# Transposing x of the last four half batches by DMA, in an attention and token-mixing kernel

## The chip, the core and the metric

The kernel runs on one core of a Trainium2 chip. The metric is the device time of one launch in microseconds. The kernel before was run three times: 123.89, 124.62 and 125.48 us, a median of 124.62.

## The reference

Linear attention with a cosine weighting of positions, and then a mixing of tokens whose weights are computed from the attention's output. B = 8 batches, H = 8 heads, S = 576 positions, D = 64, all inputs and the output in fp32.

```python
theta = np.pi / 2.0 * np.arange(S) / S
phi(x) = concat(relu(x) * cos(theta), relu(x) * sin(theta))        # per head, 128 features
kv  = einsum('bhsf,bhsd->bhfd', phi(k), v)
z   = sum(phi(k), axis=2)
num = einsum('bhsf,bhfd->bhsd', phi(q), kv)
den = einsum('bhsf,bhf->bhs', phi(q), z)[..., None] + 1e-06
x   = (num / den), heads side by side                              # B, S, 512
wq, wk = x @ w_q, x @ w_k                                          # B, S, 64
W_tok  = einsum('bsd,btd->bst', wq, wk) / sqrt(64)
out    = relu(einsum('bst,btd->bsd', W_tok, x)) @ w_out            # B, S, 512
```

The kernel never forms `W_tok`: since `W_tok @ x = wq @ (wk^T @ x)`, it computes `wk^T @ x` (64 x 512) for each batch.

## The kernel before, in words

The work of attention is cut into 16 half batches H = 0 to 15. Half batch H is batch H // 2 and four of its heads, as two pairs of heads. Each pair gives one group g = 2H or 2H + 1, so that there are 32 groups. The mixing runs once for each of the 8 batches, and the last product, by `w_out`, in 36 row tiles of 128 rows.

The order of all work is written out by hand in the string `ORDER` (line 24). Each word is a step and its index, then `:` and the place in PSUM, then `@` and the engine that copies (A for ScalarE, V for VectorE, G for GpSimd). Each engine, and each queue of transfers, does its part of the words in the order in which they stand. All transfers are issued from SyncE's queue (SP). An SP instruction that must wait holds back all that stand behind it there.

The steps that matter here, with their lines:

- `LK`, `LQ`, `LV` (`load`, line 129) bring in k, q and v, two transfers of 288 KB for each half batch. The last loads in the order are those of `LK15`.
- `N` (line 261) computes numerators and denominators of one group into PSUM, `EP` (274) adds 1e-06 to the denominators, and `X` (281) on VectorE takes the reciprocal (L286) and multiplies (L287) into the bf16 buffer `x`. `x` has two buffers, one for a batch and one for the next. Its layout is partition, `u` (5 blocks of two 64-row pieces), head, d.
- `XT` (292) and `XR` (303) transpose `x` on TensorE into PSUM. `XT` moves whole 128 x 128 blocks, 10 for a half batch (L300). `XR` moves halves of 64 partitions, 20 for a half batch (L313). Both are followed by `XE` (316), which copies the result from PSUM into the bf16 buffer `xT`, on ScalarE (L193) or VectorE (L197).
- `WK` (328) takes `xT` of both half batches of one batch, 20 matmuls (L333), and `KW` copies the result to `wk`. `KX` (355) computes `wk^T @ x` with 10 matmuls, whose moving operand is 256 columns of `x` (L360). `WQ` (341) takes `xT` as moving operand (L346). `MX` (378) and `ME` mix and apply the relu.
- `WO` (398) computes one row tile with 4 matmuls of 512 columns (L403), `OE` (406) copies it to one of 12 output buffers `o`, and `ST` (412) stores it, 256 KB each (L413).

The half batches 12 to 15 are the last four. They form the batches 6 and 7. In the order, `XR12` stands behind `N27`, and `XR13` behind `QT14`. `XE12` and `XE13` are on ScalarE, and `WK6` follows `WO19`. `XR14` and `XR15` stand together behind `X31`, the last `X`. `MX27`, `WO25` and `WK7` follow.

Of the kernel before, what the change touches and what calls it, by code (L numbers as in the profile page):

```python
# [13 lines left out]
BF16 = mybir.dt.bfloat16  # L14
# [7 lines left out]


ORDER = """
LV1 LQ0b LQ1 TK CV1@G TQ LK1 TV LV0a TI TZ LV0b T2 RK1@G RQ1@A TW VS1 LK0a CV0b@A QT1:0 RQ0b@A
LQ0a CV0a@G KV1:2 LK0b RK0a@G RQ0a@A QM1 KE1@V RK0b@A VS0a VS0b N2:4 LV3 LQ3 RQ3@A LK3 CV3@G EP2@V
N3:6 LV2 LK2 QT0:0 KV0:2 X2 EP3@A LQ2 RK3@G QM0 KE0@A VS3 N0:4 LV5 X3 QT3:0 EP0@A KV3:2 QM3 LW0
LW1 X0 CV2@G KE3@A RK2@A VS2 XT1:6 N1:0 EP1@A LK5 LQ4 X1 N6:4 CV5@G LQ5 XE1@A RQ2@A EP6@A LV7 N7:2
LV4 KV2:0 QT2:6 EP7@A LQ7 KE2@V XT0:0 X6 CW1 QM2 CW0 N5:4 XE0@A WK0:6 N4:0 RK5@A X7 RQ5@G WQ0:7
VS5 EP4@V X4 EP5@V KW0@A RQ4@A KX0:6 XR3:2 XK0@A QW0@V X5 XB0@A XE3@A XA0@A KV5:0 LK4 LQ6 KE5@A  # L30
QT5:6 LW2 XT2:4 CV7@G MX1:2 QM5 LV6 XE2@A MX3:0 QT4:6 CV4@G ME1@A ME3@A RK4@G MX2:4 VS4 LK7 QM4
WK1:2 WQ1:3 KW1@A N11:0 RQ7@G KX1:2 CW3@G N10:6 QW1@V ME2@A MX0:4 XK1@A EP11@A ME0@A VS7 X11 KV4:2
EP10@A KE4@A N9:4 X10 N8:0 RQ6@A CW4@G XT5:2 EP8@A X8 LV8 LK6 CV6@G RK7@G QT7:6 LV10 CW2@A EP9@A
X9 XA1@A CW5@A WO1:0 XE5@A LQ8 LV9 XR4:4 QT6:2 WO2:1 QM7 OE1:0@A KV7:6 XB1@G QM6 RK6@G VS6 XE4@A
MX7:2 WQ2:0 KE7@A MX4:4 ME7@A OE2:1@A N15:6 MX5:2 QW2@A ME4@V EP15@A WK2:1 N14:4 LK10 ME5@A KW2@A
KV6:2 EP14@A X15 CV8@G KE6@A MX6:0 ME6@A KX2:6 LQ9 X14 N12:2 VS8 LK8 XK2@A EP12@A N13:0 EP13@A X13
CV9@G WO7:7 RQ8@A XR7:4 QT8:0 OE7:2@A WO0:6 XE7@A XA2@G X12 RQ9@G LK9 WO5:7 OE0:3@A WO4:6 VS9
XB2@A MX9:4 QM8 XR6:2 OE5:4@A LQ11 RK8@A QT9:0 CV10@G WO6:7 RK9@G RQ11@G OE4:5@A LV11 CV11@G ME9@V
MX11:4 XE6@V KV8:2 LQ10 WK3:6 ME11@A MX10:4 OE6:6@A QM9 KV9:0 VS10 KW3@A RK10@G ME10@A KE9@A KE8@V
KX3:7 XK3@A ST6 MX8:4 XB3@V N19:0 LK11 EP19@V N18:2 ME8@A N16:6 WO11:4 LV12 RQ10@G WO3:5 X19  # L40
QT11:0 EP18@A EP16@A X18 N17:2 OE11:7@A WQ3:4 X16 XA3@A OE3:8@A EP17@A QW3@A KV10:6 X17 RK11@G
KE10@A QM11 XR9:4 CV12@G LK14 QT10:2 QM10 WO9:6 XE9@A LK13 XT8:0 WO12:7 WO8:2 OE9:9@A XE8@A WK4:3
LV13 VS11 MX12:4 OE12:10@A MX13:0 VS12 OE8:11@A N20:6 KW4@A LQ12 KV11:2 ME12@A ME13@A CV13@G
EP20@V LK12 KE11@A WO10:4 N22:0 MX15:2 X20 VS13 OE10:6@A EP22@A ME15@A MX14:6 KX4:5 WQ4:4 N23:2
RQ12@G ME14@A LQ13 XK4@A RK12@A RK13@G N21:6 EP21@A X22 XA4@G QW4@A ST10 XB4@G WO13:5 LV14 LV15
EP23@V X23 OE13:6@A KV12:0 ST13 ST4 X21 KE12@A KV13:2 LQ14 KE13@A MX17:4 ME17@A QT12:6 QM12 XR11:0
XR10:2 XE11@A RQ13@G WO17:4 QT13:6 ST3 MX16:0 LQ15 WO15:5 CV15@G ME16@A CV14@G N25:0 XE10@V ST11
OE15:6@A N24:2 QM13 ST15 EP25@V OE17:5@A MX19:6 X25 EP24@A WQ5:5 ST17 LK15 QW5@A WO14:4 RQ14@G
WK5:5 ME19@A X24 MX18:0 N27:6 XR12:2 OE14:8@A KW5@A ST5 ME18@A VS15 RQ15@G EP27@A RK15@G N26:4
KX5:0 XK5@A EP26@V WO18:1 WO16:0 X27 X26 QT15:6 QT14:4 XE12@A OE16:7@A XR13:2 WO20:0 OE18:6@A ST8  # L50
RK14@G VS14 XE13@A QM14 WO19:1 QM15 ST7 WK6:2 OE20:5@A XB5@A KV15:4 XA5@G KW6@A KV14:6 ST20 MX23:2
OE19:4@V KE15@A MX21:0 ST0 WQ6:4 ME21@A KE14@V KX6:5 ME23@V MX20:0 N30:6 MX22:2 QW6@V WO21:4
ME20@A N29:0 EP30@V ST2 ME22@A XK6@A N28:2 X30 N31:6 EP29@A EP28@A X29 X28 OE21:11@A ST12 XB6@A
WO24:5 XA6@G WO22:4 OE24:2@A WO23:5 EP31@A X31 OE22:5@A XR14:0 XR15:2 XE14@A MX27:6 OE23:3@V
WO25:4 ST18 XE15@V ST16 WK7:5 ME27@V OE25:1@A MX26:0 KW7@A ME26@A MX25:2 ST14 MX24:6 WQ7:4 KX7:5
ME24@V ME25@A WO26:0 XK7@A QW7@V XB7@A WO29:1 MX31:6 XA7@G ST22 MX28:2 ME31@A ST9 MX30:4 OE26:10@V
WO28:0 ST21 MX29:6 ST23 ST1 ME30@A OE29:6@V WO30:1 ST25 ME29@A ST19 ME28@V ST29 OE28:7@V WO32:0
ST24 WO31:4 ST26 ST28 WO33:5 OE32:8@V OE30:5@A ST32 ST30 OE31:9@A ST31 OE33:11@A WO27:6 OE27:3@A
ST33 WO35:7 ST27 OE35:0@A ST35 WO34:2 OE34:1@A ST34
"""  # L60


# [1 line left out]
def kernel(  # L64
# [10 lines left out]
    nc = tc.nc  # L75

    B, NH, S, D = q.shape
    DM = NH * D
    DH = moe_w_q.shape[1]
    P = 128  # L80
# [4 lines left out]
    SC = CP // 2  # L85
    HS = S // 2
    NDM = DM // P
# [6 lines left out]
    NRAW, NPREP, NV2, NQM, NX, NXT, NOUT = (4, 2, 2, 2, 2, 2, 12)  # L94
    XC = DM // 2
# [5 lines left out]
    def bufs(n, shape, dtype, name):  # L101
        return [pool.tile(shape, dtype, name=f"{name}{i}") for i in range(n)]
# [6 lines left out]
    qm_b = bufs(NQM, [P, 2, 2, CP, D], BF16, "qm")  # L109
    kv_b = bufs(2, [P, 2, 2, DV], BF16, "kvs")  # L110
    rec_b = bufs(8, [P, 2, SC, 1], FP32, "rec")
    x_b = bufs(NX, [P, SC, NH, D], BF16, "x")
    xT_b = bufs(NXT, [P, NDM, CP, D], BF16, "xT")
    wk_b = bufs(2, [P, SC, DH], BF16, "wk")
    wq_b = bufs(2, [P, HS], BF16, "wq")
# [23 lines left out]
    ident = pool.tile([P, P], BF16, name="ident")  # L139
# [42 lines left out]
    A, V, G = nc.scalar, nc.vector, nc.gpsimd  # L182
# [35 lines left out]
    def pair(i):  # L218
        return PS[:, i:i + 2, :]
# [38 lines left out]
    def num(t):  # L258
        return pair(t).bitcast(FP32)[:, :, 0:SC * (D + 1)].rearrange("p w (u e) -> p w u e", u=SC)
# [21 lines left out]
    def X(g, ps, eng):  # L281
        H, r = divmod(g, 2)
        b, h = divmod(H, 2)
        rec = rec_b[g % 8]
        nv = num(place["N", g])
        V.reciprocal(rec, rec)  # L286
        V.tensor_tensor(  # L287
            x_b[b % NX][:, :, 4 * h:4 * h + 4, :].rearrange(
                "p u (w r) d -> p r w u d", r=2)[:, r],
            nv[:, :, :, 0:D], rec.to_broadcast([P, 2, SC, D]), op=ALU.mult)  # L290

    def XT(H, ps, eng):
        b, h = divmod(H, 2)
        o = pair(ps).rearrange("p t e -> p (t e)").bitcast(BF16)[:, 0:2 * SC * P].rearrange(
            "p (w n) -> p w n", w=2)
        place["XT", H] = o[:, :, 0:S]
        for w in range(2):
            for u in range(SC):
                hd = 4 * h + 2 * w
                nc.tensor.transpose(o[:, w, u * P:(u + 1) * P],  # L300
                                    x_b[b % NX][:, u, hd:hd + 2, :], ident)

    def XR(H, ps, eng):
        b, h = divmod(H, 2)
        o = pair(ps).bitcast(BF16)[:, :, 0:2 * SC * D].rearrange(
            "p t (w u d) -> p w t u d", w=2, d=D)
        place["XT", H] = o
        for w in range(2):
            for u in range(SC):
                for t in range(2):  # L310
                    a = slice(H2 * t, H2 * t + H2)
                    hd = 4 * h + 2 * w
                    nc.tensor.transpose(o[:, w, t, u, :], x_b[b % NX][a, u, hd:hd + 2, :],  # L313
                                        ident[a, a])

    def XE(H, ps, eng):
        b, h = divmod(H, 2)
        dst = xT_b[b % NXT][:, 2 * h:2 * h + 2]
        o = place["XT", H]
        if len(o.shape) == 5:  # L320
            cast(eng, dst.rearrange("p w (u t) d -> p w t u d", t=2), o)
        else:
            cast(eng, dst[:, :, 0:C, :].rearrange("p w c d -> p w (c d)"), o)

    def bank(i):
        return PS[:, i, :].bitcast(FP32)
# [28 lines left out]
    def KX(b, ps, eng):  # L355
        place["KX", b] = ps
        o = bank(ps)
        for u in range(SC):
            for t in range(2):
                nc.tensor.matmul(  # L360
                    o[H2 * t:H2 * t + H2, 0:XC], wk_b[b % 2][:, u, :],
                    x_b[b % NX][:, u].rearrange("p h d -> p (h d)")[:, t * XC:(t + 1) * XC],
                    start=(u == 0), stop=(u == SC - 1))

    def XK(b, ps, eng):
# [57 lines left out]
    def CW(i, ps, eng):  # L423
        if i < 2:
            cast(eng, (wqw, wkw)[i], (wq_f, wk_f)[i])
        else:
            m = i - 2
            cast(eng, wow[:, m, :], wo_f[:, m, :])

    steps = {f.__name__: f for f in (KV, QT, KE, QM, N, EP, X, XT, XR, XE, WK, KW, WQ, QW, KX, XK, XA, XB,  # L430
                                     MX, ME, WO, OE, ST, LW, CW, TK, TV, TI, TQ, TW, T2, TZ)}
    halves = {f.__name__: f for f in (RK, RQ, CV, VS)}

    for word in ORDER.split():
        word, _, eng = word.partition("@")
        word, _, ps = word.partition(":")
# [3 lines left out]
        i, ps = int(word[len(kind):] or 0), int(ps or 0)  # L440
# [37 lines left out]
```

## Time and profile before

| | |
|---|---|
| median of three runs | 124.62 us |
| profiled execution, its own time | 122.49 us |
| span of that execution, first to last instruction | 120.7 us |
| granted TensorE clock, mean of the core | 0.991 |
| TensorE matmuls busy | 94.8 us (79%) |
| VectorE busy | 88.2 us (73%) |
| ScalarE busy | 84.2 us (70%) |
| GpSimd busy | 52.2 us (43%) |
| moved by DMA | 39.40 MB, mean 326 GB/s |
| XR's matmuls (L313) | 220, of 191 ns |
| copies into `xT` from XR | 8 on ScalarE of 1229 ns, 3 on VectorE of 817 ns |
| median from issue to landing of a store | 3.1 us |

Busy times are those of one profiled execution. Matmuls overlap each other, so that a group's busy time is less than its count times the mean of one. The lines `SPq` of a timeline are the issuing of transfers by SyncE, not the transfers themselves. The DMA share is the mean busy share of the core's 16 DMA engines, and it can lie a little above 1.

### The profile page before, as it was taken

The numbers are of one execution on the slowest core, as the hardware profiler recorded it, in microseconds if no ns is written. First come the engines' busy times: TensorE is split into PE (matmuls) and PEld (weight loads), VectorE is DVE, ScalarE is ACT, GpSimd is POOL, SyncE is SP. The second block draws the span as 40 slices with busy tenths as digits, with TensorE's granted clock in tenths as the row PEclk, the third lists the DMA queues.
The fourth block names the chain that finished last, engine by engine and source line by source line (L and its number), as shares of the span: only waits on it lengthen the run. The fifth ranks groups of instructions, "written<-read, shape, count | busy, mean of one in ns | idle before, by whom it ended". The sixth has DMA issues, their size and how long they took to land.

```text
span 120.7 us, 5301 instructions
## 1 busy us (share of the span) xinstructions
PE 94.8 (79%) x2286; PEld 63.1 (52%) x2286; DVE 88.2 (73%) x132; ACT 84.2 (70%) x155; POOL 52.2 (43%) x63
## 2 busy tenths in 40 slices
PE   0005919758778899969999999798999999999950
PEld 0004818637656656635667576454755864653410
DVE  0136998889989998997979987759969868766200
ACT  7246452967887989777967897586678668757450
POOL 2577136032739758146799304937365310010000
PEclk9999999999999999999999999999999999999996
DMA  3999999999999999999989999999997681875685
GB/s 111 318 384 405 395 391 391 361 405 396 392 390 408 398 337 344 355 360 379 383 282 326 364 285 391 343 331 283 391 299 263 238 329 55 320 288 198 237 331 196
DMA packets 20615, 39.40 MB, mean 326 GB/s; under 512 B 3184, under 2 KB 3184, under 8 KB 20592
## 3 DMA queue, kind: packets, MB, share of 16 engines
q1 hardware_dynamic: 20592, 39.07, 89.8%
q8 instruction: 18, 0.29, 1.0%
q14 instruction: 5, 0.04, 0.1%
HBM read 29.62 MB, written 9.44 MB: 324 GB/s over the span
## 4 chain that ended last, share of the span: by engine, by line
DMA 39%; PE 39%; DVE 6%; issue 4%; SPq 3%; ACT 3%; POOL 2%; DVEq 0%; ACTq 0%; POOLq 0%
DMA kraw<-in_k_dram 24%; PE ps L403 20%; DMA vraw<-in_v_dram 11%; DMA out_dram<-o 5%; PE ps L234 3%; PE ps L383 3%; PE ps L269 3%; SPq L132 3%; PE ps L360 3%; DVE v L213 2%; PE ps L313 2%; DVE x L287 2%; PE ps L245 2%; PE ps L333 2%; PE ps L346 2%
## 5 line engine op out<-in xcount | busy, mean ns | idle before, releaser
L403 PE MATMUL ps<-wow,mix 128*128 128x512 bf16 x144 | 34.7, 380 | 0.0
L287 DVE TENSOR_TENSOR x<-ps,rec 128x640 bf16<-128x640 f32 x32 | 26.4, 824 | 2.2
L195 POOL TENSOR_SCALAR vb<-vraw 128x1152 bf16<-128x1152 f32 (+1 forms) x16 | 17.9, 1122 | 20.9 <-DMA vraw<-in_v_dram 18.6
L213 DVE TENSOR_TENSOR v<-vb,vtab 128x2304 bf16<-128x2304 bf16 (+1 forms) x17 | 21.7, 1289 | 6.6 <-POOL vb L195 6.6
L253 DVE TENSOR_TENSOR qm<-ps,qtab 128x2304 bf16<-128x2304 bf16 x16 | 21.4, 1350 | 4.6 <-ACT qtab L166 2.9
L193 ACT COPY o<-ps 128x512 f32<-128x512 f32 x30 | 17.5, 587 | 6.6 <-PE ps L403 4.5
L269 PE MATMUL ps<-kvs,qm 64*128 64x65 bf16 x640 | 15.3, 199 | 6.0 <-ACT kvs L193 3.3
L403 PEld LDWEIGHTS <-mix 128*128 128x128 bf16 x144 | 12.4, 98 | 14.2 <-issue 0.9
L394 ACT ACTIVATE mix<-ps 128x576 bf16<-128x576 f32 x26 | 16.4, 657 | 3.2 <-PE ps L383 3.2
L189 POOL TENSOR_SCALAR rq<-qraw 128x1152 bf16<-128x1152 f32 x9 | 13.4, 1487 | 11.4 <-DMA qraw<-in_q_dram 10.8
L269 PEld LDWEIGHTS <-qm 64*128 64x128 bf16 x640 | 13.3, 100 | 9.4 <-issue 5.7
L189 POOL TENSOR_SCALAR rk<-kraw 128x1152 bf16<-128x1152 f32 (+1 forms) x12 | 13.8, 1150 | 9.4 <-DMA kraw<-in_k_dram 7.0
L193 ACT COPY xT<-ps 128x1280 bf16<-128x1280 bf16 (+1 forms) x13 | 15.4, 1186 | 3.3 <-PE ps L313 1.7
L234 PE MATMUL ps<-v,rk 64*64 64x130 bf16 x576 | 12.5, 236 | 3.0 <-DVE x L287 1.3
L245 PE MATMUL ps<-ident,rq 64*128 64x64 bf16 x288 | 7.6, 199 | 9.3 <-ACT rq L187 8.8
L187 ACT ACTIVATE rq<-qraw 128x1152 bf16<-128x1152 f32 (+1 forms) x8 | 8.4, 1046 | 6.6 <-DMA qraw<-in_q_dram 6.6
L234 PEld LDWEIGHTS <-rk 64*64 64x64 bf16 x576 | 10.1, 117 | 5.2 <-ACT rk L187 1.4
L245 PEld LDWEIGHTS <-rq 64*128 64x128 bf16 x288 | 6.1, 101 | 11.7 <-ACT rq L187 9.0
L383 PE MATMUL ps<-wq,kx 64*128 64x288 bf16 x64 | 8.3, 287 | 0.3 <-ACT xT L193 0.2
L195 POOL TENSOR_SCALAR kx<-kx 64x256 bf16<-64x256 bf16 x7 | 2.8, 399 | 12.6 <-ACT kx L193 12.2
L286 DVE RECIPROCAL rec<-rec 128x10 f32<-128x10 f32 x32 | 6.8, 211 | 1.8 <-ACT rec L277 1.4
L277 ACT ACTIVATE rec<-ps,eps 128x10 f32<-128x10 f32 x23 | 6.2, 273 | 1.7 <-PE ps L269 1.6
(46 smaller groups left out, 99.3 us busy)
## 6 DMA issues: line engine op xcount, KB each, us to landing
vraw<-in_v_dram SPq DMA_DIRECT2D x32, 288.0 KB, 6.0
qraw<-in_q_dram SPq DMA_DIRECT2D x32, 288.0 KB, 5.9
kraw<-in_k_dram SPq DMA_DIRECT2D x32, 288.0 KB, 5.9
out_dram<-o SPq DMA_DIRECT2D x36, 256.0 KB, 3.1
wof<-in_moe_w_out_dram SPq DMA_DIRECT2D x1, 1024.0 KB, 7.6
wqf<-in_moe_w_q_dram SPq DMA_DIRECT2D x1, 128.0 KB, 5.5
wkf<-in_moe_w_k_dram SPq DMA_DIRECT2D x1, 128.0 KB, 5.2
```

Source lines behind the costliest of these rows:

```text
L189: eng.tensor_scalar(dst, s, FMAX, 0.0, op0=ALU.min, op1=ALU.max)
L193: A.copy(dst, s)
L195: G.tensor_scalar(dst, s, 1.0, 1.0, op0=ALU.mult, op1=ALU.mult)
L213: V.tensor_mul(v2_b[H % NV2][:, part, :, :, 0:D], vb_b[H % NPREP][:, part].unsqueeze(3).to_broadcast([P, n, C, 2, D]), vtab.unsqueeze(1).t ...
L234: nc.tensor.matmul(kv_v[o, r, :], rk_b[H % NPREP][a, pr, c, :], v2_b[H % NV2][a, pr, c, :, 0:D + 1], start=(c == 0), stop=(c == C - 1))
L245: nc.tensor.transpose(qt_v[:, r, c * H2:(c + 1) * H2], rq_b[H % NPREP][a, c, :, :], ident[a, a])
L253: V.tensor_mul(qm_b[H % NQM][:, :, :, 0:C, :].rearrange("p s r c d -> p s r (c d)"), qt_view(place["QT", H]).unsqueeze(1).to_broadcast([P, ...
L269: nc.tensor.matmul(nv[:, pr, u, :], qm_b[H % NQM][a, s, r, 2 * u:2 * u + 2, :], kv_b[H % 2][a, r, s, 0:D + 1], start=(u == 0 and s == 0), ...
L287: V.tensor_tensor(x_b[b % NX][:, :, 4 * h:4 * h + 4, :].rearrange("p u (w r) d -> p r w u d", r=2)[:, r], nv[:, :, :, 0:D], rec.to_broadca ...
L383: nc.tensor.matmul(pair(ps)[:, t, :].bitcast(FP32)[:, 0:HS], kx_b[b % 2][a, (m // 2) ^ t, (m % 2) * P:(m % 2 + 1) * P], wq_b[b % 2][a, :], ...
L394: A.activation(dst, s, AF.Relu, scale=scale_moe)
L403: nc.tensor.matmul(o, mix_b[bp % 2][:, m, rt * P:(rt + 1) * P], wow[:, m, :], start=(m == 0), stop=(m == NDM - 1))
```

## The change

Two things are changed. The buffer `x` is laid out as partition, column tile (128 columns, two heads), u, r (head of the tile), d, so that the 1280 elements of a half batch lie together in a partition. `X`, `XT`, `XR` and `KX` address it accordingly. A new step `XD` transposes a half batch with one DMA from `x` to `xT`, issued from SyncE. It takes the place of `XR` and `XE` in the half batches 12 to 15. `XD12` to `XD15` stand where `XR12` to `XR15` stood, and `XE12` to `XE15` are gone. The other words of `ORDER` are the same and in the same order; those shown are the ones around the edits.

```diff
-WK5:5 ME19@A X24 MX18:0 N27:6 XR12:2 OE14:8@A KW5@A ST5 ME18@A VS15 RQ15@G EP27@A RK15@G N26:4
-KX5:0 XK5@A EP26@V WO18:1 WO16:0 X27 X26 QT15:6 QT14:4 XE12@A OE16:7@A XR13:2 WO20:0 OE18:6@A ST8
-RK14@G VS14 XE13@A QM14 WO19:1 QM15 ST7 WK6:2
...
+WK5:5 ME19@A X24 MX18:0 N27:6 XD12 OE14:8@A KW5@A ST5 ME18@A VS15 RQ15@G EP27@A RK15@G N26:4
+KX5:0 XK5@A EP26@V WO18:1 WO16:0 X27 X26 QT15:6 QT14:4 OE16:7@A XD13 WO20:0 OE18:6@A ST8
+RK14@G VS14 QM14 WO19:1 QM15 ST7 WK6:2
...
-WO24:5 XA6@G WO22:4 OE24:2@A WO23:5 EP31@A X31 OE22:5@A XR14:0 XR15:2 XE14@A MX27:6 OE23:3@V
-WO25:4 ST18 XE15@V ST16 WK7:5
...
+WO24:5 XA6@G WO22:4 OE24:2@A WO23:5 EP31@A X31 OE22:5@A XD14 XD15 MX27:6 OE23:3@V
+WO25:4 ST18 ST16 WK7:5
...
-    x_b = bufs(NX, [P, SC, NH, D], BF16, "x")
+    x_b = bufs(NX, [P, NDM, SC, 2, D], BF16, "x")
...
-            x_b[b % NX][:, :, 4 * h:4 * h + 4, :].rearrange(
-                "p u (w r) d -> p r w u d", r=2)[:, r],
+            x_b[b % NX][:, 2 * h:2 * h + 2, :, r, :],
             nv[:, :, :, 0:D], rec.to_broadcast([P, 2, SC, D]), op=ALU.mult)
...
-                hd = 4 * h + 2 * w
                 nc.tensor.transpose(o[:, w, u * P:(u + 1) * P],
-                                    x_b[b % NX][:, u, hd:hd + 2, :], ident)
+                                    x_b[b % NX][:, 2 * h + w, u, :, :], ident)
...
-                    hd = 4 * h + 2 * w
-                    nc.tensor.transpose(o[:, w, t, u, :], x_b[b % NX][a, u, hd:hd + 2, :],
+                    nc.tensor.transpose(o[:, w, t, u, :], x_b[b % NX][a, 2 * h + w, u, :, :],
                                         ident[a, a])
+
+    def XD(H, ps, eng):
+        b, h = divmod(H, 2)
+        nc.sync.dma_start_transpose(
+            xT_b[b % NXT][:, 2 * h:2 * h + 2].rearrange("p w (u t) d -> p (w u) (t d)", t=2),
+            x_b[b % NX][:, 2 * h:2 * h + 2].rearrange("p w u r d -> p (w u r d)"))
...
-                    x_b[b % NX][:, u].rearrange("p h d -> p (h d)")[:, t * XC:(t + 1) * XC],
+                    x_b[b % NX][:, 2 * t:2 * t + 2, u].rearrange("p m r d -> p m (r d)"),
                     start=(u == 0), stop=(u == SC - 1))
```

On SyncE's queue `XD12` comes behind the two transfers of `LK15`, then the store of row tile 5, `XD13`, and the stores of row tiles 8 and 7. `XD14` and `XD15` come behind the store of row tile 12 and ahead of those of 18, 16 and 14.

## The prediction

> **What bounds the kernel now.** I read the page's slices and queue table first, then the chain of waits, then the timeline and the stretches of 84 to 105 us, where all edited steps lie. The page:
>
> ```profile
> DMA  3999999999999999999989999999997681875685
> ...
> q1 hardware_dynamic: 20592, 39.07, 89.8%
> ...
> L313 PE MATMUL ps<-ident,x 64*128 64x64 bf16 x220 | 5.2, 191 | 1.0 <-issue 1.0
> ```
>
> The transfers fill the first three quarters (nines up to slice 30, about 91 us) and then leave gaps; the rest of the end belongs to TensorE. The chain in order of time (start, length, what) says so:
>
> ```profile
> 102.48 0.40 PE ps L313 x20
> 102.88 0.03 issue
> 102.90 0.47 PE ps L313 x20
> 103.37 0.12 PE ps L383 x2
> 103.49 0.97 PE ps L403 x4
> 104.46 0.58 PE ps L333 x20
> ```
>
> From 88.53 to 116.34 us the chain stands on TensorE with hardly a gap, so whatever delays a matmul there moves the end by as much. L313 is XR, L333 is WK, its first reader. The timeline (start, busy, engine, line) gives what a transfer in XR's place waits for, and when WK wants its result:
>
> ```profile
> 86.30 1.75 SPq L132 DMA_DIRECT2D kraw<-in_k_dram  x1
> ...
> 89.90 0.83 DVE L287 TENSOR_TENSOR x<-ps,rec 128x640 bf16<-128x640 f32 x1
> ...
> 93.69 0.75 PE L333 MATMUL ps<-wkw,xT 128*128 128x64 bf16 x20
> ...
> 102.02 0.82 DVE L287 TENSOR_TENSOR x<-ps,rec 128x640 bf16<-128x640 f32 x1
> ...
> 104.29 0.75 PE L333 MATMUL ps<-wkw,xT 128*128 128x64 bf16 x20
> ```
>
> X26, the last x of batch 6, ends at 90.73 and WK6 starts at 93.69: 2.96 us. X28, the last but one x of batch 7, ends at 101.70 (0.82 from 100.88), X31 at 102.84, and WK7 starts at 104.29: 1.45 us after X31. The stretches (length, engines, clock, DMA share, GB/s) show the rings:
>
> ```profile
> 22.00:23.00 1.00, 1.00 (x38) 0.85 (x32) 0.90 (x3) 1.00 (x3) 0.00 (x0) 1.00 1.09 300
> 23.00:24.00 1.00, 0.23 (x16) 0.24 (x17) 0.65 (x1) 1.00 (x2) 0.00 (x0) 1.00 1.12 368
> 24.00:25.00 1.00, 0.94 (x54) 0.72 (x43) 0.44 (x2) 0.84 (x3) 0.83 (x1) 1.00 1.06 406
> ...
> 101.00:102.00 1.00, 1.00 (x6) 0.49 (x5) 0.92 (x2) 0.97 (x3) 0.00 (x0) 1.00 0.01 2
> ```
>
> Around 102 us the queue is empty. Between 92 and 93 us its share is 0.47 and after that 0.06: it drains at about 92.5.
>
> **What goes.** 80 transposes and 4 copies. On the chain XR13 is 0.29 us, XR14 0.40, XR15 0.47; XR12 lies beside other waits (0.45 us busy at 87.17). Some 1.5 us of TensorE at most, and that is the most the change can gain: the copies (three of 1.23 us on ScalarE, one of 0.82 on VectorE) only delay WK, which now waits for something else.
>
> **What stays.** X, XT, XR and KX address x by column tile. X keeps 128x640 pieces in runs of 64, KX 256 moving columns (now two runs of 128): taken at nothing; the 276 ns of a KX matmul and 824 ns of an X show no other layout, so a few per cent either way on them (8 x 10 and 32 of them) is not excluded.
>
> **What comes.** Four transfers of 128 x 1280 bf16, 0.328 MB read and written, on SP's queue. The trace has no transposing transfer. Call the time that one holds the rings T.
> - Low end: the copy rate, 406 GB/s at 24 to 25 us, gives 0.81 us.
> - Nearest row: the two small weight loads, 0.262 MB in runs of 256 bytes, as the source here is cut (128 columns of bf16), landed at 24.3 and 24.7. At 22 to 24 us the rate fell to 300 and 368 GB/s, 0.144 MB short of 406, or 0.36 us over the 0.65 that they would need: about 260 GB/s, T = 1.25.
> - High end: 89.8% of 16 engines' 120.7 us over 20,592 packets is 84 ns a packet, mostly of 2 KB. 1280 runs over 16 engines are 80 each: 6.7 us.
> I take 1.25 + 0.81 = 2.1 us: a block is read in short runs, and written again after it is read. It is an estimate, nearest to the second row.
>
> The Trainium skill, "Advanced Engine Details and Errata", section X-Bar Transpose (TRN2), says transposing transfers are as fast as regular ones, 350 to 400 GB/s; by it T would be 0.82 to 0.94. No run shown here tests that.
>
> Batch 6. XD12 needs X24 (done at 86.10) but stands behind the last k load, issued until 88.05. The three stores issued next, from 88.10 on, hold 0.79 MB, 2.0 us at 390 GB/s, and drain at 92.5: so k drains at 90.45, and lands near 91.8, a receipt of 1.3 us. Now XD12 follows k, then one store (0.65), then XD13, issued once X26 is done at 90.73. WK6 starts at 90.45 + T + 0.65 + T + 1.3 = 92.4 + 2T, against 93.69: 2T - 1.3, or +2.9 us. The 0.7 us that XR12 and XR13 leave on TensorE vanish in this wait. With no cover WK6 blocks all matmuls behind it: KV15, KV14, MX, WQ6.
>
> Batch 7. XD14 waits for X28, XD15 for X31, on idle rings. The fastest store landed 2.1 us after its issue, 0.65 of it moving: 1.45 fixed. Both have landed at 101.70 + 1.45 + 2T, later than 102.84 + 1.45 + T once T is over 1.14. Against 104.29 that is 2T - 1.14, +3.1 us on top of the shift; between X31 and WK7 stand only MX27 and WO25, 1.2 us of TensorE. The sum is 4T - 2.4 = +6.0 us: 122.49 would be 128.5. The profiled execution lies 2.1 us under the median, so 130.6 there.
>
> SP waits in order: behind XD13 stand the stores of row tiles 8 and 7, behind XD14 and XD15 those of 18, 16, 14, issued by 98.5 before and now after 104. Their buffers are wanted by OE21 at about 99.9, OE24, and from 109 on by OE28, OE29 and OE32; I cost this at nothing. If that cover went, see the third rival.
>
> **The rivals.**
> 1. Copy rate: T is 0.81. WK6 slips by 0.3; WK7 comes with X31, 102.84 + 1.45 + T, so the sum is 3T - 1.3 = +1.1, 125.8: not slower. For it: plain transfers hold 390 to 406 GB/s. Against: even 256-byte runs do not. It decides below T = 1.2, where 4T - 2.4 is 2%. At T near nothing 1.5 us could be gained. Chance 0.22, 0.02 of it faster by over 2%.
> 2. Run by run: T is 6.7, each short run costing what a packet of 2 KB does. 4T - 2.4 = +24.4, 149.0. For it: a 32-byte piece per column and block on the write side, which no row prices. Against: the 256-byte loads. Chance 0.15 for T over 4. The Trainium skill, "VectorE: DVE Perf Modes", section The three transpose paths, speaks against the change with 1309 ns for a 128x128 block by DMA and 390 by TensorE; ten blocks one after another would be 13.1 us and the sum +50. The trace has TensorE's side only, 238 ns for a full block's transpose.
> 3. Stores: three held back stores, 2.0 us of rings, land after their buffers are wanted, and output copies, then TensorE, wait: 6.0 + 2.0, 132.6. Against: ScalarE waited for stores only 1.4 us in all after 78 us, and the last 28 matmuls drain 12 buffers. Chance 0.05.
>
> **How the numbers follow.** The forecast, T from 1.2 to 4, has 0.58 and gives 130.6. A measurement of this kernel tells about 2% (2.5 us) from no change. Slower: 0.58 + 0.15 + 0.05 = 0.78; within: 0.20; faster: 0.02. The range takes T from 0.9 (3T - 1.3 = +1.4) to 4.5 (+15.6): 126.0 to 140.2; it leaves out the fast part of rival 1 and most of rival 2. The forecast alone spans 127.1 to 138.2.
>
> **What would show it.** L313 has 140 matmuls instead of 220. WK6 and WK7 start right after a transfer into xT lands, and TensorE idles before each, about 3.6 us before WK6 (2.9 and the 0.7 not used), 4 before WK7. The issue list has four transfers xT<-x; landing in batch 7 of 1.45 + T. If TensorE has no such gaps, or xT lands within 2.3 us of X31, T is wrong and rival 1 right. If SP is busy for microseconds issuing each one, then my T is really SP's. If ScalarE waits for stores after 105 us, rival 3 has come in.

## The result, and the profile after

| | before | after |
|---|---|---|
| median of four runs on one chip | 125.05 us | 132.05 us (130.25 to 132.79) |
| ratio, 95% interval | | 1.059 [1.048, 1.070] |
| profiled execution | 122.49 us, span 120.7 | 130.25 us, span 128.5 |

The four runs of before are the three given at the start and a fourth of 126.45 us. Executions come in a faster and a slower state, and ratios, here and below, are of runs in the faster one, so that they are not quotients of the medians.

The kernel is slower by about 6%. The page of the changed kernel (slices; a group with its count, busy us and mean ns, idle us and what ended it; queue table; issues with median us to landing) answers the lines shown of before:

```profile
PEclk9999999999999999999999999999997799869999
...
DMA  4999999999999999999899998699999204997794
...
q1 hardware_dynamic: 25840, 40.38, 90.9%
...
L302 PE MATMUL ps<-wkw,xT 128*128 128x64 bf16 x160 | 6.6, 196 | 5.6 <-DMA xT<-x 5.4
...
xT<-x SPq DMA_TRANSPOSE x4, 4.8
```

WK (now L302) waits 5.4 us for transfers into `xT`, and the clock, at 9 through the same slices of before, drops twice, to 7 and 7 and to 8 and 6. The chain of waits, in order of time (start, length, what):

```profile
90.71 6.40 DMA xT<-x
97.15 0.70 PE ps L302 x18
97.85 2.10 PE ps L200 x61
...
108.06 3.08 DMA xT<-x
111.18 0.97 PE ps L302 x18
```

TensorE's solid stretch has two holes, and both end with a transfer, from its issue to its landing. The timeline (start, busy, engine, line; in brackets the idle time ahead and what ended it):

```profile
87.59 2.38 SPq L281 DMA_TRANSPOSE xT<-x  x1
...
90.71 2.56 SPq L281 DMA_TRANSPOSE xT<-x  x1
...
92.94 2.26 POOL L155 TENSOR_SCALAR rk<-kraw 128x1152 bf16<-128x1152 f32 x2 [2.21 <-DMA kraw<-in_k_dram]
...
94.08 0.23 PE L302 MATMUL ps<-wkw,xT 128*128 128x64 bf16 x2 [0.66 <-DMA xT<-x]
...
97.15 0.70 PE L302 MATMUL ps<-wkw,xT 128*128 128x64 bf16 x18 [2.83 <-DMA xT<-x]
...
106.64 2.69 SPq L281 DMA_TRANSPOSE xT<-x  x2
...
107.81 0.30 PE L352 MATMUL ps<-wq,kx 64*128 64x288 bf16 x2 [0.43 <-DVE x L253]
...
109.79 0.23 PE L302 MATMUL ps<-wkw,xT 128*128 128x64 bf16 x2 [0.71 <-DMA xT<-x]
...
111.18 0.97 PE L302 MATMUL ps<-wkw,xT 128*128 128x64 bf16 x18 [1.16 <-DMA xT<-x]
```

WK6 runs two matmuls on the first half and waits 2.83 us for the second. WK7 does the same. The 18 matmuls of WK7 take 0.97 us, those of WK6 0.70: the clock. Where the 7.8 us of span went can be read from five marks: the end of X26, the start of the last 18 or 20 matmuls of WK6, the end of X28, the same of WK7, the last matmul. The table has the time between marks in one profiled execution of each kernel. The lower rows are experiments told below. e1_layout has no transfer in it, and its first two stretches are 0.48 and 0.81 us longer than those of before: so much can differ without any transfer.

| us | X26 to WK6 | WK6 to X28 | X28 to WK7 | WK7 to last matmul | to the end |
|---|---|---|---|---|---|
| before | 2.96 | 8.01 | 2.59 | 12.05 | 4.36 |
| after | 6.66 | 9.46 | 4.57 | 13.55 | 3.77 |
| e1_layout | 3.44 | 8.82 | 2.59 | 12.03 | 4.05 |
| e7_fill | 6.53 | 7.96 | 4.55 | 11.99 | 4.20 |
| e4_copy | 4.25 | 7.97 | 3.66 | 11.99 | 4.50 |
| e6_beside | 2.87 | 9.59 | 2.60 | 12.03 | 6.72 |
| e5_none | 2.67 | 9.13 | 2.31 | 12.03 | 3.54 |

The last 18 matmuls of WK6 start 3.46 us after the start of WK6 in before (97.15 against 93.69; X26 ended 0.24 earlier), the stretch behind it is 1.45 longer, WK7's wait 1.98, the stretch behind that 1.50, and the tail 0.59 shorter: 7.80. The two stretches of 1.45 and 1.50 hold no wait that was not there before. They are the clock, as the stretches of time show (length; busy us of PE, PEld, DVE, ACT, POOL; clock; DMA share; GB/s), cut where the clock changes:

```profile
94.36:97.77 3.41, 0.62 (x18) 0.58 (x18) 0.81 (x2) 0.00 (x0) 1.23 (x2) 1.00 1.22 220
97.77:101.18 3.41, 3.41 (x85) 2.60 (x84) 1.18 (x2) 1.38 (x3) 0.00 (x0) 0.50 0.81 310
101.18:104.60 3.42, 3.37 (x101) 2.33 (x98) 1.85 (x5) 1.98 (x7) 0.40 (x1) 1.00 0.02 5
...
108.01:111.42 3.41, 1.54 (x16) 0.67 (x15) 1.01 (x2) 0.59 (x1) 0.00 (x0) 1.00 1.08 278
111.42:114.84 3.42, 3.42 (x40) 2.32 (x36) 1.22 (x2) 1.55 (x3) 0.00 (x0) 0.50 1.03 377
```

TensorE's matmuls were idle for 2.79 us of the first stretch shown and 1.87 of the fourth. The stretch after each ran at half clock, for 3.41 us. A mechanism that the prediction did not have thus cost 2.95 us of the 7.8.

### The profile page after: what moved, and what is told of

Read it like the earlier page. It is cut to its first block, busy times and chain, and to the rows that moved or that the text cites. A ratio compares the mean times of both kernels' runs of the same rounds, so it can differ in the third digit from the quotient of the medians.

```text
span 128.5 us, 5130 instructions
## 1 busy us (share of the span) xinstructions
PE 95.7 (75%) x2192; PEld 63.9 (50%) x2206; DVE 89.2 (69%) x131; ACT 80.6 (63%) x152; POOL 54.0 (42%) x63
## 4 chain that ended last, share of the span: by engine, by line
DMA 36%; PE 32%; DVE 10%; issue 5%; ACT 5%; SPq 5%; POOL 3%; DVEq 0%; ACTq 0%; POOLq 0%
DMA kraw<-in_k_dram 19%; PE ps L372 12%; DMA vraw<-in_v_dram 10%; DMA xT<-x 7%; SPq L98 5%; PE ps L200 4%; DVE v L179 4%; PE ps L352 3%; DVE x L253 3%; PE ps L235 3%; PE ps L315 3%; PE ps L302 2%; PE ps L329 2%; ACT rk L153 2%; POOL rq L155 1%
## 5 line engine op out<-in xcount | busy, mean ns | idle before, releaser
L372 PE MATMUL ps<-wow,mix 128*128 128x512 bf16 x130 | 33.3, 380 | 1.2 <-issue 0.5
L179 DVE TENSOR_TENSOR v<-vb,vtab 128x2304 bf16<-128x2304 bf16 (+1 forms) x17 | 23.3, 1380 | 8.4 <-POOL vb L161 6.0
L161 POOL TENSOR_SCALAR vb<-vraw 128x1152 bf16<-128x1152 f32 (+1 forms) x16 | 18.8, 1175 | 20.1 <-DMA vraw<-in_v_dram 19.3
L155 POOL TENSOR_SCALAR rk<-kraw 128x1152 bf16<-128x1152 f32 (+1 forms) x12 | 14.3, 1193 | 10.2 <-DMA kraw<-in_k_dram 10.2
L155 POOL TENSOR_SCALAR rq<-qraw 128x1152 bf16<-128x1152 f32 x9 | 13.8, 1531 | 9.4 <-DMA qraw<-in_q_dram 7.8
L200 PE MATMUL ps<-v,rk 64*64 64x130 bf16 x576 | 13.6, 248 | 4.0 <-ACT rk L153 1.9
L200 PEld LDWEIGHTS <-rk 64*64 64x64 bf16 x576 | 11.1, 124 | 6.4 <-ACT rk L153 2.6
L159 ACT COPY xT<-ps 128x1152 bf16<-128x1152 bf16 (+1 forms) x10 | 11.7, 1172 | 1.2 <-PE ps L264 1.2
L302 PE MATMUL ps<-wkw,xT 128*128 128x64 bf16 x160 | 6.6, 196 | 5.6 <-DMA xT<-x 5.4
L302 PEld LDWEIGHTS <-xT 128*128 128x128 bf16 x160 | 5.7, 100 | 7.7 <-DMA xT<-x 6.6
L352 PE MATMUL ps<-wq,kx 64*128 64x288 bf16 x64 | 8.8, 310 | 0.7 <-DVE x L253 0.4
```

The source lines that it names most:

```text
L155: eng.tensor_scalar(dst, s, FMAX, 0.0, op0=ALU.min, op1=ALU.max)
L159: A.copy(dst, s)
L161: G.tensor_scalar(dst, s, 1.0, 1.0, op0=ALU.mult, op1=ALU.mult)
L179: V.tensor_mul(v2_b[H % NV2][:, part, :, :, 0:D], vb_b[H % NPREP][:, part].unsqueeze(3).to_broadcast([P, n, C, 2, D]), vtab.unsqueeze(1).t ...
L200: nc.tensor.matmul(kv_v[o, r, :], rk_b[H % NPREP][a, pr, c, :], v2_b[H % NV2][a, pr, c, :, 0:D + 1], start=(c == 0), stop=(c == C - 1))
L302: nc.tensor.matmul(o[:, u * DH:(u + 1) * DH], xT_b[b % NXT][:, m, 2 * u:2 * u + 2, :], wkw[:, m, :], start=(m == 0), stop=(m == NDM - 1))
```

## The experiments

Diffs are against the changed kernel. Ratios are against the kernel before, run on the same chip.

**The layout alone: e1_layout.** XR and XE of before come back in their old places; x keeps the new layout.

```diff
-N27:6 XD12 OE14:8@A
+N27:6 XR12:2 OE14:8@A
-QT14:4 OE16:7@A XD13 WO20:0
+QT14:4 XE12@A OE16:7@A XR13:2 WO20:0
-RK14@G VS14 QM14
+RK14@G VS14 XE13@A QM14
-XD14 XD15 MX27:6
+XR14:0 XR15:2 XE14@A MX27:6
-ST18 ST16 WK7:5
+ST18 XE15@V ST16 WK7:5
```

> Only the layout of x is changed; all half batches are transposed by TensorE as before. My theory (the price is the wait for the four transfers, and the layout costs nothing): the time of before within 1%, X still 824 ns, KX still 276 ns, XR 191 ns. The rival that the layout slows X or KX: over 1% slower, with one of these means up by some per cent.

Measured: 1.014 [0.991, 1.036], 124.95 us against 124.13. X took 825 ns (824 before), a KX matmul 275 (276). The instructions of the layout cost the same, and the loss isn't there. The interval is too wide to say it to within 1%.

**A plain copy in the transfer's place: e4_copy.**

```diff
-        nc.sync.dma_start_transpose(
-            xT_b[b % NXT][:, 2 * h:2 * h + 2].rearrange("p w (u t) d -> p (w u) (t d)", t=2),
+        nc.sync.dma_start(
+            xT_b[b % NXT][:, 2 * h:2 * h + 2].rearrange("p w c d -> p (w c d)"),
             x_b[b % NX][:, 2 * h:2 * h + 2].rearrange("p w u r d -> p (w u r d)"))
```

> The four transfers move the same bytes from x to xT at the same places in the order, but as plain copies; xT of the batches 6 and 7 then holds x untransposed. My theory (the transposing form is dearer than a copy: dead time on the rings, about 290 GB/s, longer issue): the sum at the copy rate, +1.1 to +2.5 us against before, a ratio of 1.01 to 1.02; rings without dead stretches between 90 and 97 us. The rival (any transfer in this place costs it: the round trip from X to WK and the queue ahead): +6 to +8 us, as with the transposing ones.

Measured: 127.19 us against 124.13, runs scattered from 124.59 to 131.46, no ratio given; so the profile has to carry it (124.59 us, 2.1 above the profiled 122.49). The timeline, and one microsecond of the rings where the second copy runs:

```profile
94.69 0.70 PE L302 MATMUL ps<-wkw,xT 128*128 128x64 bf16 x18 [1.22 <-DMA xT<-x]
...
106.32 0.70 PE L302 MATMUL ps<-wkw,xT 128*128 128x64 bf16 x18 [0.91 <-DMA xT<-x]
```

```profile
92.00:93.00 1.00, 0.95 (x5) 0.39 (x4) 1.00 (x2) 0.54 (x1) 0.43 (x1) 1.00 1.07 410
```

WK still waits, though the data now move at the rate of any copy. By the table, WK6 is 1.0 us late (94.69 against 93.69) and X28 to WK7 1.07 longer: 2.1 us is the price of any transfer in this place, in this one execution. Of the 1.0, some 0.7 may be the last k, on which GpSimd started at 92.57, in before at 91.91 (see e5_none). What is transposing about it costs the rest of the waits, 2.46 at WK6 and 0.91 at WK7. With the shorter waits of the copy the clock stays at 1.00: no 2.95.

**No transposition at all: e5_none.** The four XD are gone, WK and WQ of these batches read what lies in `xT`.

```diff
-N27:6 XD12 OE14:8@A
+N27:6 OE14:8@A
-OE16:7@A XD13 WO20:0
+OE16:7@A WO20:0
-XD14 XD15 MX27:6
+MX27:6
```

> Neither XR and XE nor the transfers run for the batches 6 and 7; WK and WQ read the xT of the batches 4 and 5. This is the most that taking XR and XE away can give. My theory (TensorE carries the end of the chain): 1.0 to 1.6 us under before, a ratio of 0.987 to 0.992. The rival (the transposes were hidden in the end anyway, so that nothing could be gained): the time of before within 0.5 us.

Measured: 0.991 [0.962, 1.019]; its profiled execution is 0.6 us below that of before, where 1.5 us had been the ceiling. In the table WK6 and WK7 gain 0.29 and 0.28 and the stretch between gives 1.12 back. The timeline says to whom (L200 is KV, L155 the relu of k on GpSimd; the line of before, with L189 for that relu, stands below):

```profile
93.10 2.26 POOL L155 TENSOR_SCALAR rk<-kraw 128x1152 bf16<-128x1152 f32 x2 [3.22 <-DMA kraw<-in_k_dram]
...
94.30 0.72 PE L200 MATMUL ps<-v,rk 64*64 64x130 bf16 x36 [0.47 <-POOL rk L155]
95.41 0.72 PE L200 MATMUL ps<-v,rk 64*64 64x130 bf16 x36 [0.39 <-POOL rk L155]
```

```profile
91.91 2.26 POOL L189 TENSOR_SCALAR rk<-kraw 128x1152 bf16<-128x1152 f32 x2 [2.23 <-DMA kraw<-in_k_dram]
```

KV waits for the last k, which reached GpSimd 1.19 us later in this execution than in that of before. The changed kernel has it 1.03 later (92.94), and this kernel, which has no transfer there, shows that such lateness comes without one. With the k of before, its relu would have been done by 94.17, and KV would hardly have waited; how often it is late was not measured. At WK7 the gain is only 0.28, though XR14 and XR15 were 0.87 us of the chain, because `MX27` then waits for X31 (0.43 us, as in the changed kernel at 107.81). So by these marks even a transfer that cost nothing would have gained about 0.6 us here.

**Keeping TensorE busy in the wait: e7_fill.** Products of the identity with `w_out`, read by nobody, are put ahead of WK6 (13 matmuls) and WK7 (7).

```diff
+    def FL(n, ps, eng):
+        for _ in range(n):
+            nc.tensor.matmul(bank(ps), ident, wow[:, 0, :], start=True, stop=True)
...
-WK6:2
+FL13:2 WK6:2
...
-WK7:5
+FL7:5 WK7:5
```

> The changed kernel with 13 extra matmuls ahead of WK6 and 7 ahead of WK7 (into the bank that WK overwrites), which only fill the wait. My theory that 2.9 to 3 us of the loss are matmuls at half clock after the two waits: faster than the changed kernel by 2 to 3 us (a ratio to before of 1.035 to 1.045), granted clock 1.00 in the stretches after both waits, and the landing of xT as before. The rival that the clock has no part: the time of the changed kernel, 1.059, or more where the extra matmuls delay WK.

Measured: 1.055 [1.036, 1.074], over the 1.035 to 1.045 expected and not apart from the changed kernel's 1.059. The profiled execution does not settle it by its time: GpSimd started on the last k 2.6 us later (95.55 against 92.94) and its marks start 2.9 us later (X26 at 93.36 against 90.49), before the first added matmul. Between the marks the two stretches behind the waits are 7.96 and 11.99 us, those of before to 0.1 us, with the waits ahead unchanged (6.53 and 4.55). The stretches of time cut at the clock's grid:

```profile
96.25:99.67 3.42, 2.91 (x16) 1.27 (x13) 1.60 (x2) 0.27 (x1) 1.95 (x3) 1.00 1.29 202
99.67:103.08 3.41, 3.19 (x112) 2.69 (x112) 1.27 (x3) 1.46 (x3) 0.00 (x0) 1.00 1.04 396
```

Idle 0.51 us in place of 2.79, then a full clock. That the half clock comes from the idle time of TensorE, and costs 3 us by the marks, is shown; that filling it pays in the whole run is not.

**One batch at a time: e2_batch6 and e3_batch7.** XD in batch 6 alone, with XR and XE in batch 7, and the other way round (the words of e1_layout, half of them each).

> Only XD12 and XD13 are taken over; batch 7 is transposed by TensorE as before. My theory (each batch pays its own wait and then some 3.5 us of half clock): WK6 ends its wait about 3.5 us late and 1.4 us more are lost behind it; 4 to 5 us over before, a ratio of 1.03 to 1.04. The rival that only the last batch counts, because batch 6 has time in hand: within 1% of before.

> Only XD14 and XD15 are taken over; batch 6 is transposed by TensorE. My theory: WK7 waits 2 us more and 1.5 us go to half clock behind it; 3 to 3.5 us over before, a ratio of 1.02 to 1.03, and the two batches add up to the whole change. The rival that only the last batch counts: the whole 1.055 to 1.06 here.

Measured: 1.013 [0.995, 1.032] and 1.007 [0.994, 1.021]. Both are less than expected (1.03 to 1.04 and 1.02 to 1.03), and together about 2% against the 5.9% of the change: the parts do not add. Part of the reason is in e3_batch7's profile, timeline and stretches at the clock's grid:

```profile
107.82 0.70 PE L302 MATMUL ps<-wkw,xT 128*128 128x64 bf16 x18 [1.19 <-DMA xT<-x]
```

```profile
103.23:106.65 3.42, 2.23 (x12) 0.64 (x10) 2.26 (x4) 1.08 (x2) 0.00 (x0) 1.00 0.65 148
106.65:110.06 3.41, 2.24 (x42) 1.71 (x42) 1.03 (x2) 1.51 (x3) 0.00 (x0) 1.00 1.04 352
```

X28 to WK7 is 4.64 us (4.57 in the changed kernel), so the wait is the same. But the grid's border falls inside it, each side has 1.2 us idle, and no half clock follows: 0.70 us for 18 matmuls, not 0.97. Where the borders lie differs between executions (the first change of the clock comes at 13.9 to 27.5 us in the fourteen that were profiled), so this accounts for some of the missing 4%; how much was not measured.

**Hiding the wait by order: e8_reorder, with its control e9_reorder_xr.** WK6 goes behind N29, WK7 behind MX24 (`WQ6` and `KX6` move back too); in the control XR and XE stand in the same order.

```diff
-ST7 WK6:2 OE20:5@A
+ST7 OE20:5@A
...
-EP30@V ST2 ME22@A XK6@A N28:2
+EP30@V ST2 ME22@A WK6:5 KW6@A N28:2
...
-ST18 ST16 WK7:5 ME27@V
+ST18 ST16 ME27@V
...
-ME24@V ME25@A WO26:0
+ME24@V ME25@A WK7:5 KW7@A WQ7:4 KX7:5 WO26:0
```

> The changed kernel with other work moved ahead of the two waits: WK6, KW6, WQ6 and KX6 behind N29 and N31, WK7 behind MX25 and MX24. All of the computation stays. My theory (the wait is the price, so work put into it takes it away): TensorE without gaps of over 1 us between 95 us and the end, no half clock there, a ratio to before of 0.985 to 1.00. The rival (the transfers themselves, by their dead time on the rings or by SP held back, cost the time wherever WK stands): over 1.02.

> The same other order with the transposes and copies of before in place of the four transfers: the control for the order alone. My theory: the order by itself is worth little, 0.99 to 1.00, and lies level with the reordered kernel that transposes by DMA or up to 0.8% above it (the 0.9 us of XR14 and XR15 on TensorE). If it lies 2% below that one, the transfers cost something besides the wait.

Measured: 1.049 [1.036, 1.062] and 1.021 [1.010, 1.032]. WK6 no longer waited (WK7 still did, 1.13 us), and yet most of the loss stayed: a miss. The control lies 2.6% lower, so that by the expectation's own rule the transfers cost something besides the wait of WK6. A piece of the chain that ends in the next wait (L281 is XD12):

```profile
91.17 0.67 SPq L281
91.84 0.06 issue
91.90 5.45 DMA out_dram<-o
...
97.44 0.70 DVE o L163
```

The store of row tile 5 was issued only at 91.90, behind the 2.22 us in which SP issued XD12, and landed 5.45 us later. In the control the same store was issued at 89.05 and took 5.0 us, without any transposing transfer: it is the issue that came late, more than the landing. An output copy on VectorE waited 1.62 us for its buffer, and behind it mixing, and TensorE. The new order is also worse by itself, by the 2.1% of the control.

**The four transfers beside XR: e6_beside.** XR and XE do the work; the four transfers run too, into a spare buffer.

```diff
+    xs_b = bufs(NXT, [P, NDM, CP, D], BF16, "xs")
...
-N27:6 XD12 OE14:8@A
+N27:6 XD12 XR12:2 OE14:8@A
...
-            xT_b[b % NXT][:, 2 * h:2 * h + 2].rearrange("p w (u t) d -> p (w u) (t d)", t=2),
+            xs_b[b % NXT][:, 2 * h:2 * h + 2].rearrange("p w (u t) d -> p (w u) (t d)", t=2),
```

> XR and XE transpose all half batches as before, and the four transposing transfers run as well, at their places, into a spare buffer that nothing reads. My theory (the price is that WK waits for their landing): 0 to 1.2 us over before, a ratio of 1.00 to 1.01. The rival (the transfers cost the time by what they do to the rings and to SP: dead stretches, a store in between that lands late, the last k load): 1.03 or more with no wait of WK for a transfer.

Measured: 1.029 [1.009, 1.050]: my theory missed. Nobody waits for `xs`, WK6 and WK7 come on time, and still the table has 1.58 us more between WK6 and X28 and 2.36 more at the end. The timeline and the last stretch:

```profile
96.25 1.06 PE L201 MATMUL ps<-v,rk 64*64 64x130 bf16 x36 [0.39 <-POOL rk L156]
...
97.18 0.69 DVE L164 COPY o<-ps 128x512 f32<-128x512 f32 x1 [1.89 <-DMA out_dram<-o]
...
103.98 2.69 SPq L282 DMA_TRANSPOSE xs<-x  x2
106.73 14.28 SPq L383 DMA_DIRECT2D out_dram<-o  x21
```

```profile
120.00:122.00 2.00, 0.00 (x0) 0.00 (x0) 0.00 (x0) 0.00 (x0) 0.00 (x0) 1.00 1.01 384
```

Of the 1.58, 1.0 us is KV waiting for the relu of the last k (it ends 2.95 us after the start of WK6, 1.92 in before); e1_layout has that wait too, so it is not shown to be the transfers' doing. The other 0.55 is the late store again, the second line. Then SP stands before XD14 until X28 is done, the 21 stores behind it start only after XD15, at 106.73, and they are still draining at full rate when every engine is finished. The late store and the held back stores are two costs of the transfers that are no wait for their data. In the changed kernel the same output copy waited 1.75 us, inside the wait of WK6, and the second is masked: TensorE is itself so late that the stores catch up (tail 3.77).

**The store out of the way: e10_st5.** The store of row tile 5 goes right behind the last k load, so that XD12 and XD13 are neighbours in the queue.

```diff
-KW5@A ST5 ME18@A
+KW5@A ME18@A
...
-WQ5:5 ST17 LK15 QW5
+WQ5:5 ST17 LK15 ST5 QW5
```

> The changed kernel with the store of row tile 5 issued ahead of XD12, not between XD12 and XD13, so that the two transfers follow each other on the rings. If a dead stretch of 1.1 to 1.2 us stands ahead of each transposing transfer that finds plain transfers ahead of it, one of the two in batch 6 goes: XD13 lands within 2 us of XD12 (3.1 in the changed kernel), and the whole is some 1 us faster than the changed kernel, 1.045 to 1.055. The rival that each one drains the rings whatever is ahead: 3 us between the landings, and 1.055 to 1.06.

Measured: 1.073 [1.055, 1.092]. The landings came 0.9 us apart, as expected of neighbours, but not sooner; a miss. The rings (stretches of one microsecond) show that the data were not what took the time:

```profile
94.00:95.00 1.00, 1.00 (x6) 0.39 (x4) 1.00 (x1) 0.53 (x1) 0.21 (x1) 1.00 0.29 45
96.50:97.50 1.00, 0.00 (x0) 0.00 (x0) 0.50 (x1) 0.00 (x0) 0.92 (x2) 1.00 0.05 5
```

Each transfer has a dead stretch in its middle. The changed kernel has the same, and the trace's packets say more. The changed kernel's view of transfers from 94 to 96 us (40 slices), and from 107.8 to 110.6, each with its table of queues:

```profile
GB/s 533 312 271 276 241 297 261 276 261 179 26 15 20 10 0 0 0 0 0 0 0 10 10 5 10 5 10 10 5 15 5 10 10 10 10 10 15 148 287 282
...
q8 instruction: 1, 0.02, 3.3%
```

```profile
GB/s 55 179 267 289 293 293 278 293 293 293 289 293 289 293 282 293 257 129 30 0 7 91 201 227 267 293 293 293 285 293 282 293 289 293 285 293 293 268 323 337
...
q1 hardware_dynamic: 2637, 0.69, 107.6%
```

A transposing transfer is 1280 packets of 256 bytes, 18 ns each on 16 engines, at 290 GB/s. On rings of their own (batch 7) XD14 and XD15 run through in 1.3 us each. XD13 starts as fast, and 0.45 us in, about one packet on each engine takes 1.2 to 1.4 us; in XD12 20 packets take 1.0 to 1.4. In seven traces, this was there in each of the 13 transfers during which a load was moving (the last k load for XD12, a 16 KB load of instructions for XD13), and in none of the other 13, among them XD13 of e11_hide, where a load starts only in its last 0.1 us. The dead stretch ended 0.2 to 1.4 us after the load did. A store is not needed for it: none moved during that of XD13 in e2_batch6 and in e10_st5. e4_copy's plain transfers ran through beside the same loads. This is an association over traces: no run took the loads away, and of the 13 without a dead stretch all but the one in e11_hide stand in batch 7.

**Both together: e11_hide, with its control e12_hide_xr.** The store of row tile 5 moved as above, WK6 behind X30, WK7 behind OE26; the control has XR and XE in this order.

```diff
-ST7 WK6:2 OE20:5@A
+ST7 OE20:5@A
...
+EP30@V X30 WK6:5 KW6@A MX20:0 WQ6:4 KX6:5 MX22:2
...
-ST18 ST16 WK7:5 ME27@V
+ST18 ST16 ME27@V
...
+OE26:10@V WK7:5 KW7@A WQ7:4 KX7:5 WO29:1
```

> The changed kernel with that store moved and a second other order: WK6 behind KV15, KV14, MX23, MX21 and N30 (which wait for the last k load anyway), WK7 behind MX26, MX25, MX24 and WO26, and WO28 earlier. The computation is whole. My theory: X31 is not late any more, no wait over 1 us ahead of WK6 or WK7, 0.99 to 1.01 of before. If the price is in the transfers themselves: over 1.03.

> The control: the order of the second reordered kernel with XR and XE in place of the transfers. My theory: 0.99 to 1.01, within 1% of the one with the transfers. A ratio 2% or more under that one would say that the transfers cost something besides the wait that was filled.

Measured: 1.019 [0.997, 1.041] and 1.024 [0.999, 1.048]. The timeline of e11_hide has neither WK waiting:

```profile
99.61 0.76 PE L302 MATMUL ps<-wkw,xT 128*128 128x64 bf16 x20
...
110.46 0.75 PE L302 MATMUL ps<-wkw,xT 128*128 128x64 bf16 x20
```

Once the readers stand far enough behind, the transfers and XR are not told apart, within intervals of about 2% either way. By their ratios both lie outside the 0.99 to 1.01 expected; that the order costs about 2% is likely, not shown, since both intervals reach 1.00. No kernel here that does the whole work was faster than the one before.

## Why the prediction was right, and where it was not

The forecast, 130.6 with a range of 126.0 to 140.2, held the 132.05, and its mechanism is the one that the chain shows: WK waits from issue to landing, with nothing to cover it. The size was partly luck: of the profiled 7.80 against the 6.0 of the sum, 2.95 is a cost that the sum does not have, and what it does have came out smaller, 4.85 with the shorter tail.

- *WK6, +2.9; measured +3.46.* TensorE was idle 3.49 us ahead of it, 3.6 were named. The drain of the rings, the store between and the second T are all in it. But 1.0 of the 3.46 may be the last k, for which XD12 waits in the queue: GpSimd started on it at 92.94, in before at 91.91, and in e5_none, without a transfer, at 93.10.
- *Batch 7, +3.1; measured +1.98.* This term was mis-sized. TensorE was idle 1.87 us ahead of WK7, where 4 were named. From the end of X28 both had landed after 4.53 us; with the 1.45 fixed that leaves 1.54 for each transfer, not 2.1.
- *T = 1.25 + 0.81.* The failed step. The 256-byte row was the right one (1.3 us of packets at 290 GB/s), but no run shows a second pass for the write: XD14's packets end at about 109.1 in the view above, and the matmuls that wait for it start at 109.79. In batch 6 the dead stretch took its place (2T there was 97.15 - 92.4, so T was 2.4, or 1.9 if 1.0 us is the late k), in batch 7 there was only SP's issuing, 1.3 us each, nearly as long as the data. One T for busy and for idle rings was too simple; the errors of the two terms, +0.6 and -1.1, partly cancel.
- *Missing: the clock.* No term stood for what TensorE does after a wait. It is 2.95 us of the profiled 7.8, more than the whole error of the sum, 1.8.
- *At most 1.5 us to gain.* Too high. TensorE did bound this stretch, but X31 was close behind XR14 and XR15: the marks of e5_none gain 0.29 and 0.28. Its last k came late as well, 0.86 us of waits that need not come in every execution.
- *The layout at nothing.* It held for the instructions: 825 and 275 ns. The time of the whole is known to within 2% only.
- *Rival 1, the copy rate, +1.1.* e4_copy is that case, and its profile gives +2.1, or +1.4 without the 0.7 that may be its later k. The rate did not come, and had it come the change would still have lost.
- *Rival 2, 84 ns a run.* A run of 256 bytes took 18 ns. The Trainium skill's 1309 ns for a block ("VectorE: DVE Perf Modes", The three transpose paths) is not a price that adds up either: ten blocks moved in 1.3 us on idle rings.
- *Rival 3, held back stores.* ScalarE did not wait for them after 105 us, save 0.28 us twice near the end (once before). The mechanism is real all the same: e6_beside has it alone, with 2.4 us at the end and 0.55 for a late store. The cover that the prediction counted on was the lateness of TensorE itself.
- *"As fast as regular ones."* The Trainium skill's rule ("Advanced Engine Details and Errata", X-Bar Transpose (TRN2)) is not borne out here: 290 GB/s on rings of their own, against 410 of the copy, and with a load alongside 0.3 MB took 2.6 to 2.8 us.

What stays open: whether and why a load stops a transposing transfer; how often the last k comes as late as in the changed kernel's profile; how the 5.9% splits, since batch 6 and batch 7 alone make 2%; and whether an order exists that hides the transfers at no cost of its own.

## What to carry to other kernels

A transfer in an engine's place pays only where its reader has the whole way from issue to landing in hand, here 3.1 us on idle rings and 6.4 on busy ones, and where the queue behind the waiting issue can spare that time. Price what comes after a wait too: the clock, the stores that pile up, the next resource that is just as late. And before a saving is counted, take the work away altogether: e5_none would have shown that there was little over half a microsecond to win.

## What the runs showed of the hardware

The clock changed on a grid of 3.41 us in all fourteen profiled executions: the lengths between changes are multiples of it. They hold 421 such stretches after the first change. In 27 of them TensorE's matmuls were idle for 1.70 us or more, and each time the next stretch had half the clock. Of the others that ran at full clock, only one (1.66 us idle) was followed by half. The count leaves out the last whole stretch of each execution, and among these is one exception: 1.76 us idle in e4_copy from 116.66 on, and full clock behind it. So about half a stretch of idle time was enough, in one piece or in several, and the same wait costs 1.5 us or nothing by where the border falls (the changed kernel against e3_batch7). The Trainium skill ("TensorE: Matmul & The Clock Gate", Part 1: The HAM clock gate) has the free-running window of 3413 ns, which agrees, but asks for a whole window without work; here 1.87 us of idle time did it.

On SP, issuing a transposing transfer took 2.38 and 2.56 us on busy rings and 1.3 on idle ones, against 0.47 to 1.22 for e4_copy's.
